# One 768 KB load of q cut in two, two softmax products on GpSimd, and a new order for the first two batches

## The chip, the cores and the metric

The kernel runs on one core of one Trainium2 chip. The metric is the device time of one launch in microseconds (us); the median of several launches is given. Kernels are compared only within the same rounds. A ratio is the mean time of one kernel's runs over that of the other's in the same rounds, so it is not quite the ratio of the medians quoted. Engines in the profile: PE is TensorE, DVE is VectorE, ACT is ScalarE, POOL is GpSimd, SP is SyncE, which only issues loads and stores here (SPq, ACTq: the issuing queues). The profiled span leaves out some 1.8 us of the launch.

## The reference, cut to what matters

```python
# q, k, v: (8 batches, 8 heads, 576, 64); w_in (512, 2048); w_out (2048, 512); beta (2048)
q_s = softmax(q over the 64 columns)          # exp, sum, divide
k_s = softmax(k over the 576 rows)
kv  = einsum('bhsd,bhse->bhde', k_s, v)
x   = einsum('bhsd,bhde->bhse', q_s, kv)      # then (8*576, 512)
h   = x @ w_in
out = (h / (1 + exp(-beta * h))) @ w_out
```

## The kernel before: what the change touches

The kernel is written in a manual order: each engine runs its instructions in the order of the program text. After a startup for batches 0 and 1 it goes through the batches with one long stream of matmuls, `h` (x times w_in) and `acc` (the gate's result times w_out), 0.216 us each. The eight heads of a batch are handled in four pairs, 0 to 3; q of one pair is 256 KB, k or v of one pair 288 KB.

```python
def load_q(b, parts=1, only=None, eng=nc.sync):      # parts `only` of b's heads, in 1 KB runs
    ...
    eng.dma_start(t[:, hs, :], src[:, hs, :])
def kz_exp(b, j):   # exponential of k, pair j of heads, on ScalarE
def vz_cast(b, j, eng, m=1, part=None):              # v to bf16
def q_exp(b, s, n): # ScalarE    def q_sum(b, s, n): # VectorE: sum, reciprocal
def q_mul(b, s, n=2, eng=nc.vector):                 # the softmax product
def tpe(b, j, tag): # 4 transposes on TensorE        def q_ev(b, j, eng): # copy out of PSUM
def kvz_mm(b, j, tag=None, n=1):                     # 18 small matmuls, k^T v of one pair
def xpe(c, j, tag): # x of one pair                  def hpe(c, j, kts): # h, one block of columns
def warm(n, tag):   # n dummy matmuls whose result nobody reads
...
load_q(0, 4, [0])                        # SyncE's queue, 256 KB
load_q(0, 4, [1, 2, 3], nc.scalar)       # ScalarE's queue, 768 KB
load_kv(k_st, k, 0, "k_st", whole=True)  # SyncE's queue, 1152 KB in 2.3 KB runs
load_kv(v_st, v, 0, "v_st", [0])         # 288 KB a pair
... # v's other pairs, beta (8 KB), w_in, w_out, batch 1
warm(18, tag="b0")
q_exp(0, 0, 4)
q_sum(0, 0, 4)
q_exp(0, 3, 4)
q_mul(0, 0, 4)
...
tpe(0, 0, "acc3")
...
warm(10, tag="acc2")
tpe(0, 2, "acc3")
... # some 215 more lines for batches 0 and 1
```

The softmax here doesn't subtract the row's maximum and nothing guards it: scores larger than these inputs give would overflow.

## Time and profile before

| | |
|---|---|
| median of 4 runs | 282.6 us (282.36 to 282.81) |
| profiled span | 280.75 us |
| first h matmul | 14.42 us |
| first h matmul to the first kv matmul of batch 2 | 46.74 us |
| from there to the end of the last matmul | 216.45 us |
| after it | 3.14 us |

The last four rows add up to the span. They come from the matmuls' times in the trace. The prediction below shows the profile's lines. In a row of digits, each digit is the busy share of one of 40 equal slices of the span, in tenths (9 is 90% or more). In a row of a timeline, the figures are start and length in us, then engine, line, operation, what is written and read, how many, and in brackets how long the engine sat idle before it and for whom it waited. Among the names, q_st, k_st and v_st are the loaded inputs, eq and ek their exponentials, rq the sums of q, va v in bf16, tp the transposes and w_in_b and w_out_b the weights in bf16. A load lands when the semaphore that tells of its end is seen.

### The profile page before, as it was taken

What the parts mean: (1) busy time and instruction counts of PE and PEld (TensorE: products, weight loads), DVE (VectorE), ACT (ScalarE), POOL (GpSimd) and SP (SyncE); (2) the same over time, 40 slices, a digit from 0 to 9 for tenths busy, and PEclk for the clock granted to TensorE, in tenths of its full rate; (3) what the DMA queues carried; (4) which work ended last, traced back from release to release, by engine and by line L of the source; (5) the groups of instructions that cost most, each with busy time, mean ns of one, the idle gap of its engine ahead of it and who ended that gap; (6) DMA issues with size and microseconds to landing.
All of it is one profiled execution on the core that took longest, in us unless ns stands there. A gap on an engine that the chain in (4) does not pass through costs nothing.

```text
span 280.8 us, 4419 instructions
## 1 busy us (share of the span) xinstructions
PE 273.9 (98%) x1699; PEld 128.2 (46%) x1728; DVE 175.3 (62%) x284; ACT 162.0 (58%) x248; POOL 38.7 (14%) x58
## 2 busy tenths in 40 slices
PE   8999999999999999999999999999999999999995
PEld 2644454444444444444444444444444544444543
DVE  3964786993498338934794469536964596354361
ACT  3767975953495439633873478337933574454451
POOL 1554237130030003000300030002100000000000
DMA  7999999929932994099309940698153034005003
GB/s 251 391 387 392 387 388 314 295 55 289 227 149 21 273 263 158 9 269 283 154 1 218 327 153 15 141 247 250 76 123 104 0 152 75 0 0 152 0 0 149
DMA packets 55172, 50.09 MB, mean 178 GB/s; under 512 B 26600, under 2 KB 47344, under 8 KB 55152
## 3 DMA queue, kind: packets, MB, share of 16 engines
q1 hardware_dynamic: 54224, 48.91, 58.3%
q10 hardware_dynamic: 928, 0.92, 0.9%
q8 instruction: 13, 0.21, 0.3%
q14 instruction: 7, 0.06, 0.1%
HBM read 36.71 MB, written 9.44 MB: 164 GB/s over the span
## 4 chain that ended last, share of the span: by engine, by line
PE 94%; DMA 3%; issue 1%; POOL 1%; SPq 0%; ACT 0%
PE h L398 44%; PE acc L446 43%; DMA v_st<-in_v_dram 3%; PE kv L339 2%; PE x L370 1%; PE acc L438 1%; PE kv L314 1%; PE x L383 1%; POOL va L171 1%; PE tp L295 0%; SPq L129 0%; SPq L106 0%; ACT o L169 0%; PE x L361 0%; PE tb L552 0%
## 5 line engine op out<-in xcount | busy, mean ns | idle before, releaser
L412 DVE SCALAR_TENSOR_TENSOR g<-th,h 128x512 bf16<-128x512 bf16 x144 | 97.0, 680 | 83.3 <-ACT th L408 81.4
L408 ACT ACTIVATE th<-h,beta_t 128x512 bf16<-128x512 f32 x144 | 97.9, 686 | 88.3 <-PE h L398 85.2
L398 PE MATMUL h<-xT,w_in_b 128*128 128x512 bf16 x569 | 141.0, 379 | 0.3
L446 PE MATMUL acc<-w_out_b,g 128*128 128x512 bf16 x538 | 136.3, 379 | 1.9 <-issue 1.1
L398 PEld LDWEIGHTS <-w_in_b 128*128 128x128 bf16 x576 | 56.3, 98 | 66.4 <-ACT w_in_b L169 0.6
L446 PEld LDWEIGHTS <-g 128*128 128x128 bf16 x560 | 53.4, 98 | 65.0 <-issue 2.5
L171 POOL CAST va<-v_st 128x2048 bf16<-128x2048 f32 (+2 forms) x14 | 17.5, 1261 | 145.7 <-DMA v_st<-in_v_dram 145.7
L259 DVE TENSOR_REDUCE rq<-eq 128x16 f32<-128x1024 bf16 (+1 forms) x20 | 22.1, 1105 | 5.6 <-ACT eq L248 5.2
L265 DVE TENSOR_TENSOR eq<-eq,rq 128x1024 bf16<-128x1024 bf16 (+1 forms) x20 | 22.8, 1142 | 0.1
L248 ACT ACTIVATE eq<-q_st 128x1024 bf16<-128x1024 f32 (+1 forms) x18 | 16.9, 956 | 3.2 <-DMA q_st<-in_q_dram 3.2
L169 ACT CAST xT<-x 128x512 bf16<-128x512 f32 x18 | 9.9, 588 | 12.1 <-PE x L370 10.1
L171 DVE CAST xT<-x 128x512 bf16<-128x512 f32 x18 | 11.6, 686 | 6.1 <-PE x L370 5.3
L171 DVE COPY o<-acc 128x512 f32<-128x512 f32 (+1 forms) x19 | 12.1, 670 | 3.3 <-PE acc L446 3.1
L169 ACT COPY o<-acc 128x512 f32<-128x512 f32 (+1 forms) x18 | 9.6, 576 | 7.5 <-PE acc L446 4.6
L190 ACT ACTIVATE ek<-k_st 128x1024 bf16<-128x1024 f32 x12 | 12.6, 1053 | 0.0
L519 PE MATMUL warm<-xT 128*128 128x512 bf16 x30 | 9.7, 483 | 1.2 <-DVE xT L600 1.2
L171 POOL CAST w_in_b<-w_in 128x512 bf16<-128x512 f32 (+1 forms) x9 | 5.9, 660 | 5.7 <-DMA w_in<-in_moe_w_in_dram 5.6
L519 PEld LDWEIGHTS <-xT 128*128 128x128 bf16 x30 | 3.4, 118 | 6.0 <-issue 3.5
L171 POOL CAST w_out_b<-w_out 128x1024 bf16<-128x1024 f32 x5 | 5.2, 1040 | 6.3 <-DMA w_out<-in_moe_w_out_dram 6.3
L183 ACT ACTIVATE ek<-k_st 128x576 bf16<-128x576 f32 x8 | 5.0, 674 | 0.6 <-DMA k_st<-in_k_dram 0.5
L260 DVE RECIPROCAL rq<-rq 128x16 f32<-128x16 f32 (+1 forms) x20 | 4.9, 243 | 0.7
L339 PEld LDWEIGHTS <-ek 128*64 128x64 bf16 x192 | 4.1, 111 | 2.5 <-issue 2.5
(48 smaller groups left out, 83.1 us busy)
## 6 DMA issues: line engine op xcount, KB each, us to landing
out_dram<-o SPq DMA_DIRECT2D x14, 512.0 KB, 3.4
q_st<-in_q_dram SPq DMA_DIRECT2D x25, 256.0 KB, 4.1
k_st<-in_k_dram SPq DMA_DIRECT2D x6, 1024.0 KB, 7.3
v_st<-in_v_dram SPq DMA_DIRECT2D x6, 1024.0 KB, 10.0
w_in<-in_moe_w_in_dram SPq DMA_DIRECT2D x6, 512.0 KB, 9.6
v_st<-in_v_dram SPq DMA_DIRECT2D x8, 288.0 KB, 8.4
w_out<-in_moe_w_out_dram SPq DMA_DIRECT2D x4, 512.0 KB, 8.8
w_out<-in_moe_w_out_dram SPq DMA_DIRECT2D x2, 1024.0 KB, 9.6
```

Source lines behind the costliest of these rows:

```text
L169: eng.copy(dst, src)
L171: eng.tensor_copy(dst, src)
L190: nc.scalar.activation(ek[b][:, :, h, :].rearrange("p i h d -> p h i d"), k_st[b][:, h, 0 : R * D].rearrange("p h (i d) -> p h i d", i=R), ...
L248: nc.scalar.activation(eq[b][:, :, s * m : (s + 1) * m, :].rearrange("p i h d -> p h i d"), q_st[b][:, s * m : (s + 1) * m, :].rearrange(" ...
L259: nc.vector.tensor_reduce(rq[b][:, 0, :, h], eq[b][:, :, h, :], axis=AX.X, op=ALU.add)
L265: eng.tensor_tensor(eq[b][:, :, h, :], eq[b][:, :, h, :], rq[b][:, 1, :, h].unsqueeze(3).to_broadcast((P, R, m, D)), ALU.mult,)
L339: nc.tensor.matmul(t[r * D : (r + 1) * D, j, :], ek[b][:, i, hd, :] if i < R else ekt[(b // 2) % 2][:, ds(hd * D, D)], va[b][:, i, hd, :] ...
L398: nc.tensor.matmul(h[:], w_unit(j, kt), x_of(c)[:, kt, :], start=(kt == 0), stop=(kt == KT - 1),)
L408: nc.scalar.activation(th[:], h_of[c, j][:], ACTF.Tanh, scale=beta_t[:, j : j + 1])
L412: nc.vector.scalar_tensor_tensor(out=g[:], in0=th_of.pop((c, j))[:], scalar=1.0, in1=h_of[c, j][:], op0=ALU.add, op1=ALU.mult)
L446: nc.tensor.matmul(acc[st][:], g[:, ds(st * P, P)], w_out_b[:, j, :], start=(j == 0), stop=(j == NJ - 1),)
L519: nc.tensor.matmul(t[:], xT[2][:, 0, 0:P], xT[2][:, 0, :])
```

## The change

Its intent: let the second pair of q land sooner, take two of VectorE's products to GpSimd, let two kv products of batch 1 share their normalisation, and reorder batches 0 and 1 around that. HB and AB in it name the memory banks that TensorE's results take in turn. The diff, cut to its core:

```diff
-    HB, AB = ["b1", "b2"], ["b0", "b3"]
+    HB, AB = ["b0", "b2"], ["b1", "b3"]
     load_q(0, 4, [0])
-    load_q(0, 4, [1, 2, 3], nc.scalar)
+    load_q(0, 4, [1], nc.scalar)
+    load_q(0, 4, [2, 3], nc.scalar)
     load_kv(k_st, k, 0, "k_st", whole=True)
     load_kv(v_st, v, 0, "v_st", [0])
+    nc.sync.dma_start(beta_r[:], ...)
+    load_kv(v_st, v, 0, "v_st", [2])
     load_kv(v_st, v, 0, "v_st", [1])
-    load_kv(v_st, v, 0, "v_st", [2])
-    nc.sync.dma_start(beta_r[:], ...)
 ...  (loads of w_in and of batch 1 in another order)
     q_exp(0, 0, 4)
+    q_exp(0, 1, 4)
     q_sum(0, 0, 4)
-    q_exp(0, 3, 4)
-    q_mul(0, 0, 4)
+    q_mul(0, 0, 4, eng=V)
+    q_exp(0, 2, 4)
+    q_sum(0, 1, 4)
+    q_exp(0, 3, 4)
+    tpe(0, 0, "acc3")
+    q_sum(0, 2, 4)
+    q_mul(0, 1, 4, eng=V)
+    q_mul(0, 2, 4, eng=G)
+    q_ev(0, 0, V)
+    warm(6, tag="acc1")
+    tpe(0, 1, "acc2")
 ...
+    q_mul(0, 3, 4, eng=G)
 ...  (the same steps of batch 0 in another order)
-    kvz_mm(1, 0, "b1", 1)
+    kvz_mm(1, 0, "b0", 2)
+    kvz_mm(1, 1)
+    kvz_norm(1, 0, 2)
 ...  (the same steps of batch 1 in another order)
```

More of the change, by code (lines that the diff above doesn't have):

```diff
@@ L562 @@
     load_q(0, 4, [0])
-    load_q(0, 4, [1, 2, 3], nc.scalar)
+    load_q(0, 4, [1], nc.scalar)
+    load_q(0, 4, [2, 3], nc.scalar)
     load_kv(k_st, k, 0, "k_st", whole=True)
     load_kv(v_st, v, 0, "v_st", [0])
+    nc.sync.dma_start(beta_r[:], moe_beta.rearrange("(hh q) -> hh q", q=2 * P))
+    load_kv(v_st, v, 0, "v_st", [2])
     load_kv(v_st, v, 0, "v_st", [1])
-    load_kv(v_st, v, 0, "v_st", [2])
-    nc.sync.dma_start(beta_r[:], moe_beta.rearrange("(hh q) -> hh q", q=2 * P))
     load_kv(v_st, v, 0, "v_st", [3])
@@ L571 @@
     w_load("in", 0, 1)
+    w_load("in", 1, 0)
     w_load("in", 0, 2)
     w_load("in", 0, 3)
-    w_load("in", 1, 0)
     w_load("in", 1, 1)
@@ L582 @@
     w_load("out", 1)
+    load_kv(v_st, v, 1, "v_st", [0])
+    load_kv(k_st, k, 1, "k_st", [0])
+    w_load("out", 2)
     load_q(1, 2, [0])
-    w_load("out", 2)
+    w_load("out", 3, 0)
     load_q(1, 2, [1])
-    load_kv(v_st, v, 1, "v_st", [2])
-    w_load("out", 3, 0)
-    load_kv(k_st, k, 1, "k_st", [0])
-    load_kv(v_st, v, 1, "v_st", [0])
-    load_kv(k_st, k, 1, "k_st", [2])
-    load_kv(k_st, k, 1, "k_st", [1])
-    load_kv(v_st, v, 1, "v_st", [1])
-    w_load("out", 3, 1)
-    load_kv(k_st, k, 1, "k_st", [3])
+    load_kv(v_st, v, 1, "v_st", [1])
+    load_kv(k_st, k, 1, "k_st", [1])
+    w_load("out", 3, 1)
+    load_kv(k_st, k, 1, "k_st", [2])
+    load_kv(k_st, k, 1, "k_st", [3])
+    load_kv(v_st, v, 1, "v_st", [2])
     load_kv(v_st, v, 1, "v_st", [3])
@@ L608 @@
     q_exp(0, 0, 4)
+    q_exp(0, 1, 4)
     q_sum(0, 0, 4)
+    q_mul(0, 0, 4, eng=V)
+    q_exp(0, 2, 4)
+    q_sum(0, 1, 4)
     q_exp(0, 3, 4)
-    q_mul(0, 0, 4)
-    q_exp(0, 2, 4)
-    q_sum(0, 3, 4)
-    tpe(0, 0, "acc3")
-    q_exp(0, 1, 4)
-    q_sum(0, 2, 4)
-    q_ev(0, 0, A)
-    q_sum(0, 1, 4)
-    q_mul(0, 2, 4)
+    tpe(0, 0, "acc3")
[5 more added lines that the diff above has]
+    tpe(0, 1, "acc2")
+    q_sum(0, 3, 4)
@@ L620 @@
     kz_exp(0, 0)
-    q_mul(0, 1, 4)
-    warm(10, tag="acc2")
+    warm(1, tag="acc1")
     tpe(0, 2, "acc3")
+    q_ev(0, 1, V)
+    q_mul(0, 3, 4, eng=G)
+    q_ev(0, 2, A)
+    warm(1, tag="acc0")
+    beta_pe("acc1")
     kz_exp(0, 1)
-    q_ev(0, 2, V)
+    vz_cast(0, 2, A, part=1)
     vz_cast(0, 0, G)
-    warm(1, tag="acc1")
-    tpe(0, 1, "acc2")
-    q_mul(0, 3, 4)
+    warm(3, tag="acc0")
+    tpe(0, 3, "acc3")
     kz_exp(0, 2)
-    warm(1, tag="acc1")
-    kvz_mm(0, 0, "acc3", 1)
+    vz_cast(0, 2, G, part=0)
@@ L633 @@
+    q_ev(0, 3, A)
+    warm(1, tag="acc0")
+    kvz_mm(0, 0, "acc2", 1)
     vz_cast(0, 1, G)
-    q_ev(0, 1, V)
-    tpe(0, 3, "acc1")
+    kvz_mm(0, 2, "acc0", 1)
     kz_exp(0, 3)
     kvz_norm(0, 0)
-    kvz_mm(0, 1, "acc2", 1)
-    vz_cast(0, 2, G)
-    q_ev(0, 3, A)
-    beta_pe("acc0")
-    kvz_norm(0, 1)
-    kvz_mm(0, 2, "acc3", 1)
-    vz_cast(0, 3, A, part=1)
-    vz_cast(0, 3, G, part=0)
-    beta_ev()
-    xpe(0, 0, "acc1")
-    kvz_norm(0, 2)
-    kvz_mm(0, 3, "acc2", 1)
-    w_castk(0, 0, G)
+    vz_cast(0, 3, G)
@@ L651 @@
+    warm(1, tag="b3")
+    kvz_mm(0, 1, "acc3", 1)
+    beta_ev()
+    kvz_norm(0, 2)
+    w_castk(0, 0, A)
+    xpe(0, 0, "acc2")
+    kvz_norm(0, 1)
+    kvz_mm(0, 3, "acc1", 1)
     xev(0, 0, A)
-    xpe(0, 1, "acc0")
+    w_castk(0, 1, G)
+    xpe(0, 2, "acc0")
     kvz_norm(0, 3)
-    xpe(0, 2, "b3")
+    xpe(0, 1, "b3")
+    xev(0, 2, A)
+    hpe(0, 1, [0], "b0")
+    hpe(0, 0, [0], "b1")
     xev(0, 1, A)
-    hpe(0, 0, [0], "b0")
-    hpe(0, 1, [0], "b1")
-    xev(0, 2, V)
-    w_castk(0, 1, A)
+    hpe(0, 2, [0], "b2")
@@ L660 @@
+    w_castk(1, 1, G)
     xpe(0, 3, "acc3")
-    w_castk(0, 2, G)
-    hpe(0, 3, [0], "b2")
-    xev(0, 3, V)
-    hpe(0, 2, [0], "acc0")
+    hpe(0, 3, [0], "acc0")
+    xev(0, 3, A)
+    hpe(0, 1, [1])
+    w_castk(1, 0, G)
     hpe(0, 0, [1])
+    hpe(0, 2, [1])
+    w_castk(0, 2, A)
+    hpe(0, 3, [1])
     w_castk(0, 3, G)
-    hpe(0, 3, [1])
-    hpe(0, 3, [2])
-    hpe(0, 1, [1])
+    hpe(0, 7, [0], "b3")
+    hpe(0, 4, [0], "acc1")
+    hpe(0, 0, [2])
+    hpe(0, 0, [3])
+    hpe(0, 2, [2])
@@ L670 @@
+    th_act(0, 0)
+    hpe(0, 4, [1])
+    hpe(0, 3, [2])
+    w_castk(1, 3, G)
+    hpe(0, 3, [3])
+    hpe(0, 2, [3])
+    g_dve(0, 0)
+    w_castk(1, 2, G)
+    th_act(0, 3)
+    hpe(0, 7, [1])
     hpe(0, 1, [2])
     hpe(0, 1, [3])
-    hpe(0, 3, [3])
-    th_act(0, 1)
-    w_castk(1, 0, G)
-    hpe(0, 0, [2])
-    hpe(0, 0, [3])
-    hpe(0, 2, [1])
-    w_castk(1, 1, G)
-    th_act(0, 3)
-    hpe(0, 2, [2])
-    g_dve(0, 1)
-    hpe(0, 2, [3])
-    hpe(0, 4, [0], "b3")
-    th_act(0, 0)
-    hpe(0, 4, [1])
@@ L686 @@
-    g_dve(0, 3)
-    w_castk(1, 3, G)
-    hpe(0, 5, [0], "b1")
-    hpe(0, 5, [1])
-    w_castk(1, 2, A)
-    g_dve(0, 0)
-    hpe(0, 7, [0], "b2")
-    th_act(0, 2)
-    hpe(0, 7, [1])
-    hpe(0, 4, [2])
-    hpe(0, 5, [2])
+    th_act(0, 2)
+    hpe(0, 7, [2])
+    g_dve(0, 3)
+    hpe(0, 4, [2])
+    hpe(0, 5, [0], "b1")
+    th_act(0, 1)
     hpe(0, 4, [3])
     g_dve(0, 2)
-    hpe(0, 5, [3])
-    th_act(0, 4)
-    hpe(0, 7, [2])
-    hpe(0, 7, [3])
-    hpe(0, 6, [0], "b0")
-    w_cast("out", 0, 0, G)
+    hpe(0, 7, [3])
@@ L705 @@
+    w_cast("out", 0, 0, G)
+    hpe(0, 5, [1])
+    th_act(0, 4)
+    g_dve(0, 1)
+    hpe(0, 5, [2])
+    hpe(0, 5, [3])
+    th_act(0, 7)
+    hpe(0, 6, [0], "b2")
+    g_dve(0, 4)
+    hpe(0, 6, [1])
+    hpe(0, 6, [2])
     th_act(0, 5)
-    hpe(0, 6, [1])
-    g_dve(0, 4)
-    hpe(0, 6, [2])
+    w_cast("out", 0, 1, G)
     hpe(0, 6, [3])
-    th_act(0, 7)
-    g_dve(0, 5)
+    g_dve(0, 7)
     mm_b(0, 0)
     th_act(0, 6)
-    w_cast("out", 0, 1, G)
-    g_dve(0, 7)
+    g_dve(0, 5)
     mm_b(0, 1)
+    w_castk(2, 0, G)
@@ L717 @@
     g_dve(0, 6)
-    w_castk(2, 0, A)
     w_castk(2, 1, G)
     mm_b(0, 2)
-    mm_b(0, 3)
     w_castk(2, 2, A)
     w_castk(2, 3, G)
-    hpe(0, 11, [0, 1, 2, 3], "b0")
+    mm_b(0, 3)
+    hpe(0, 8, [0, 1, 2, 3], "b0")
     w_cast("in", 3, 1, A)
     hpe(0, 10, [0, 1, 2, 3], "b1")
+    th_act(0, 8)
+    w_cast("in", 3, 0, G)
+    hpe(0, 11, [0, 1, 2, 3], "b2")
+    th_act(0, 10)
+    g_dve(0, 8)
+    hpe(0, 9, [0, 1, 2, 3], "b3")
+    g_dve(0, 10)
     th_act(0, 11)
-    hpe(0, 8, [0, 1, 2, 3], "b2")
@@ L729 @@
-    w_cast("in", 3, 0, G)
-    th_act(0, 10)
+    hpe(0, 13, [0, 1, 2, 3], "b0")
     g_dve(0, 11)
-    hpe(0, 9, [0, 1, 2, 3], "b3")
-    th_act(0, 8)
-    g_dve(0, 10)
-    hpe(0, 13, [0, 1, 2, 3], "b0")
-    g_dve(0, 8)
     th_act(0, 9)
-    hpe(0, 14, [0, 1, 2, 3], "b1")
+    w_cast("out", 1, 0, G)
+    hpe(0, 12, [0, 1, 2, 3], "b1")
     g_dve(0, 9)
     th_act(0, 13)
-    w_cast("out", 1, 0, G)
-    w_cast("out", 1, 1, A)
-    hpe(0, 15, [0, 1, 2, 3], "b2")
-    g_dve(0, 13)
-    mm_b(0, 4)
@@ L746 @@
-    th_act(0, 14)
-    th_act(0, 15)
-    g_dve(0, 14)
-    mm_b(0, 5)
-    q_exp(1, 0)
-    g_dve(0, 15)
-    mm_b(0, 6)
-    q_sum(1, 0)
-    mm_b(0, 7)
-    w_cast("out", 2, 1, A)
-    w_cast("out", 2, 0, G)
-    hpe(0, 12, [0, 1, 2, 3], "b0")
-    q_mul(1, 0)
-    q_exp(1, 1)
-    mm_b(0, 8)
-    vz_cast(1, 2, G, part=0)
-    vz_cast(1, 2, A, part=1)
-    mm_b(0, 9)
-    q_sum(1, 1)
-    th_act(0, 12)
-    tpe(1, 0, "b1")
-    w_cast("out", 3, 0, A)
-    tpe(1, 1, "b2")
-    mm_b(0, 10)
-    q_ev(1, 0, V)
@@ L771 @@
-    q_mul(1, 1)
-    kz_exp(1, 0)
-    mm_b(0, 11)
-    vz_cast(1, 0, G, part=0)
-    vz_cast(1, 0, A, part=1)
-    q_ev(1, 1, A)
-    g_dve(0, 12)
-    kvz_mm(1, 0, "b1", 1)
-    kz_exp(1, 2)
-    tpe(1, 3, "b3")
-    kvz_norm(1, 0)
-    tpe(1, 2, "b2")
-    mm_b(0, 12)
-    kz_exp(1, 1)
-    q_ev(1, 3, V)
-    q_ev(1, 2, V)
-    kvz_mm(1, 2, "b0", 1)
-    vz_cast(1, 1, A, part=1)
-    vz_cast(1, 1, G, part=0)
-    xpe(1, 0, "b1")
-    kvz_norm(1, 2)
-    kvz_mm(1, 1, "b2", 1)
-    xev(1, 0, A)
@@ L794 @@
-    mm_b(0, 13)
-    kvz_norm(1, 1)
-    w_cast("out", 3, 1, G)
-    hpe(1, 0, [0], "b0")
-    xpe(1, 2, "b1")
-    kz_exp(1, 3)
-    xpe(1, 1, "b2")
-    xev(1, 2, V)
-    mm_b(0, 14)
+    vz_cast(1, 0, A, part=1)
+    hpe(0, 14, [0, 1, 2, 3], "b2")
+    w_cast("out", 1, 1, G)
+    g_dve(0, 13)
+    th_act(0, 12)
+    kz_exp(1, 0)
+    mm_b(0, 4)
+    g_dve(0, 12)
+    vz_cast(1, 0, G, part=0)
+    th_act(0, 14)
+    mm_b(0, 5)
+    g_dve(0, 14)
+    mm_b(0, 6)
+    w_cast("out", 2, 0, G)
+    mm_b(0, 7)
@@ new lines @@
+    w_cast("out", 2, 1, G)
+    mm_b(0, 8)
+    q_exp(1, 0)
+    mm_b(0, 9)
+    q_sum(1, 0)
+    w_cast("out", 3, 0, G)
+    mm_b(0, 10)
+    mm_b(0, 11)
+    q_mul(1, 0, eng=V)
+    q_exp(1, 1)
+    mm_b(0, 12)
+    vz_cast(1, 1, G)
+    q_sum(1, 1)
+    mm_b(0, 13)
+    kz_exp(1, 1)
+    tpe(1, 0, "b0")
+    tpe(1, 1, "b1")
+    q_ev(1, 0, V)
+    hpe(0, 15, [0, 1, 2, 3], "b2")
+    q_ev(1, 1, A)
+    w_cast("out", 3, 1, G)
+    q_mul(1, 1, eng=V)
+    kvz_mm(1, 0, "b0", 2)
+    kz_exp(1, 2)
@@ L803 @@
+    kvz_mm(1, 1)
+    th_act(0, 15)
+    tpe(1, 2, "b1")
+    kvz_norm(1, 0, 2)
+    tpe(1, 3, "b3")
+    mm_b(0, 14)
+    q_ev(1, 2, A)
+    q_ev(1, 3, V)
+    vz_cast(1, 2, G)
+    kz_exp(1, 3)
+    g_dve(0, 15)
+    xpe(1, 0, "b0")
+    xpe(1, 1, "b1")
     vz_cast(1, 3, A, part=1)
     vz_cast(1, 3, G, part=0)
+    kvz_mm(1, 2, "b3", 1)
     xev(1, 1, V)
-    kvz_mm(1, 3, "b1", 1)
+    xev(1, 0, A)
+    kvz_mm(1, 3, "b2", 1)
     mm_b(0, 15)
+    kvz_norm(1, 2)
     kvz_norm(1, 3)
-    hpe(1, 2, [0], "b2")
+    xpe(1, 2, "b0")
@@ L810 @@
     store(0, 0)
-    xpe(1, 3, "b1")
+    hpe(1, 0, [0], "b1")
+    xev(1, 2, V)
+    hpe(1, 0, [1])
+    xpe(1, 3, "b2")
     hpe(1, 1, [0], "b3")
+    store(0, 1)
+    xev(1, 3, A)
     hpe(1, 1, [1])
-    xev(1, 3, A)
-    store(0, 1)
     hpe(1, 1, [2])
-    hpe(1, 0, [1])
     hpe(1, 0, [2])
@@ L821 @@
     hpe(1, 1, [3])
-    hpe(1, 3, [0], "b1")
+    hpe(1, 2, [0], "b0")
     th_act(1, 0)
     store(0, 3)
-    hpe(1, 3, [1])
-    hpe(1, 3, [2])
-    hpe(1, 3, [3])
-    th_act(1, 1)
-    g_dve(1, 0)
     hpe(1, 2, [1])
     hpe(1, 2, [2])
+    th_act(1, 1)
+    hpe(1, 2, [3])
+    g_dve(1, 0)
+    hpe(1, 3, [0], "b2")
+    hpe(1, 3, [1])
+    th_act(1, 2)
+    hpe(1, 3, [2])
+    g_dve(1, 1)
+    hpe(1, 3, [3])
+    mm_b(1, 0)
     th_act(1, 3)
-    hpe(1, 2, [3])
-    g_dve(1, 1)
-    mm_b(1, 0)
-    th_act(1, 2)
+    g_dve(1, 2)
+    mm_b(1, 1)
     g_dve(1, 3)
-    mm_b(1, 1)
-    g_dve(1, 2)
     tail_zero(0)
```

## The prediction

> **What bounds the kernel now.** I read, in this order: the busy shares and slices of the page, the chain of work that ended last (first 20 us), and each engine's timeline over the first 25 us and over 25 to 50 us, since the diff touches only batches 0 and 1.
>
> ```profile
> PE 273.9 (98%) x1699; PEld 128.2 (46%) x1728; DVE 175.3 (62%) x284; ACT 162.0 (58%) x248; POOL 38.7 (14%) x58
> ...
> PE   8999999999999999999999999999999999999995
> ...
> DMA  7999999929932994099309940698153034005003
> ```
>
> See: TensorE is at nine tenths or more in every slice between the first and the last; the DMA engines are full for the first eight slices (7 us each, so to 56 us).
>
> ```profile
> 1.74 8.15 DMA v_st<-in_v_dram
> 9.95 2.12 POOL va L171 x2
> ...
> 12.11 0.48 PE kv L314 x18
> ...
> 14.86 0.38 PE x L383
> 15.23 3.96 PE h L398 x18
> ```
>
> See: until 12.1 us the end hangs on the first loads of v and on two GpSimd casts (2.12 us together); from 12.11 us on the chain is TensorE's own work.
>
> ```profile
> 1.19 6.67 PE L519 MATMUL warm<-xT 128*128 128x512 bf16 x18 [1.19 <-DVE xT L600]
> 7.69 0.39 PE L295 MATMUL tp<-identity,eq 128*128 128x128 bf16 x4
> 7.92 2.32 PE L519 MATMUL warm<-xT 128*128 128x512 bf16 x10
> ...
> 12.11 0.48 PE L314 MATMUL kv<-va,ek 64*64 64x65 bf16 x18
> ...
> 14.42 0.38 PE L398 MATMUL h<-xT,w_in_b 128*128 128x512 bf16 x1
> ...
> 15.07 6.88 PE L398 MATMUL h<-xT,w_in_b 128*128 128x512 bf16 x30
> ```
>
> See: 28 of the first matmuls are dummies (warm). No idle bracket stands behind any later row. In the chain four matmuls of 512 columns take 0.86 us, so 0.216 us each; the rows from 25.24 to 46.83 us hold 86 such (18.6 us), 16 transposes (0.9) and 72 kv matmuls (1.6): 21.1 of 21.6 us. So batch 1's startup has at most 0.5 us to give back, and the rest of the time can only fall if TensorE begins its real work before 12.1 us.
>
> ```profile
> 3.79 0.63 ACT L248 ACTIVATE eq<-q_st 128x512 bf16<-128x512 f32 x1 [1.25 <-DMA q_st<-in_q_dram]
> 6.13 1.67 ACT L248 ACTIVATE eq<-q_st 128x512 bf16<-128x512 f32 x3 [1.70 <-DMA q_st<-in_q_dram]
> ...
> 9.18 2.40 ACT L183 ACTIVATE ek<-k_st 128x576 bf16<-128x576 f32 x4 [0.48 <-DMA k_st<-in_k_dram]
> ...
> 9.95 3.11 POOL L171 CAST va<-v_st 128x576 bf16<-128x576 f32 x4 [7.99 <-DMA v_st<-in_v_dram]
> ```
>
> See: the landings. q in two steps (3.8 and 6.1 us), k at 9.2, v's first pair at 9.9; v's later pairs land at 10.6, 11.4 and 12.15 by their semaphores in the trace.
>
> **What the Trainium skill says.** "DMA: Bandwidth & Descriptors", section "Issuing engines are not separate DMA queues": loads issued from several engines run on the same 16 DMA engines and interleave. The trace agrees on the sum (390 GB/s from 2.5 us on, whatever queue), so splitting a load moves no later landing forward: the last v still lands near 12.1 us. But it does not interleave finely here: the first packet of q's 768 KB from ScalarE's queue starts at 2.63 us, k's first on the other queue only at 5.03 us though it was issued at 1.24 us. Loads went one after the other in order of issue. "GPSIMD Engine Reference", section "3.1 Elementwise — side-by-side cycle accounting": a two-input product costs about 2.6 cycles an element. With 512 elements at 1.2 GHz I estimate 1.1 us and a little dispatch, 1.2 us, against 0.69 us for the same product on VectorE in the trace; the kernel before has no such GpSimd product. "SBUF — State Buffer", section "Who interferes with whom": a VectorE instruction with two SBUF inputs blocks a GpSimd instruction that reads SBUF. The trace agrees: the two GpSimd casts beside VectorE's products and copies took 1.02 and 1.14 us, the next of the same shape 0.66 us.
>
> **The change, part by part.** (1) q of batch 0 comes as 256, 256 and 512 KB. Pair 1 should land near 4.2 us instead of 6.1 (256 KB at 0.39 MB per us is 0.7 us behind the first's last packets at 3.4, and 0.1 to 0.4 us to the semaphore). If the last 512 KB still goes ahead of k, pairs 2 and 3 land at 6.1 as before. (2) Two of four products go to GpSimd. (3) Pair 2's v is loaded before pair 1's and its cast is split with ScalarE, so that VectorE and GpSimd are less in the way. (4) All four casts of x are on ScalarE now. (5) Dummies: 31 for 30, no cost while TensorE waits anyway; one (0.216 us) stands between kv products.
>
> Placing the new order by the durations of before, with q landing at 3.8, 4.2 and 6.1:
> VectorE: sums and product of pair 0 to 6.1 as before; sum of pair 1 to 6.85; of pair 2 6.8 to 7.7; product of pair 1 to 8.3; sum of pair 3 to about 9.45.
> GpSimd: product of pair 2 held up by VectorE's to about 8.3, then to 9.5; product of pair 3 9.5 to 10.7; casts of v: pair 0 10.7 to 11.35 (before: 10.97), half of pair 2 to 11.75, pair 1 to 12.4, pair 3 to 13.0.
> ScalarE: k exponential 0 at 9.18, copy of transpose 2 at 10.05, exponential 1 at 10.55, half cast at 11.1, exponential 2 at 11.55 to 12.15, copy at 12.1, exponential 3 at 12.6 to 13.2, beta, weight cast to 13.9, then x casts 0, 2, 1, 3 end at 14.4, 15.0, 15.5, 16.0.
> TensorE: kv of pair 0 at 11.45, pair 2 at 12.2, pair 1 at 12.85, x0 13.25, pair 3 13.55, x2 14.0, x1 14.2, h from 14.5, with one wait of about 0.1 us at 15.5 for x1's cast.
> By 17.1 us this gives 4 x and 11 h matmuls; before, (17.1 - 15.13)/0.216 = 9 plus 2 of 14.4 to 14.9, so 11 h as well. The startup gain is nil: what the early q gains is in front of v's landing, which didn't move, and GpSimd's two products (2.4 us) use it up. I charge +0.1 us, with 0.3 either way.
>
> Batch 1: kv of pairs 0 and 1 lie side by side, with one reciprocal for two: VectorE saves three small instructions of 0.17 to 0.23 us, off the path. Two switches fewer between 512-column matmuls and kv (starts 0.31 us apart where 0.216 is usual in the trace) give 2 x 0.09 = 0.2 us. Against it, v of pairs 2 and 3 now lands last (42.5 to 43.8 us by the same total of bytes) and kv of pairs 2 and 3 is due near 43.9: cast of 0.5 to 1.1 us, so a wait of 0.1 to 0.4 us. Sum -0.2 + 0.25: nil. From batch 2 on, both kernels have the same instructions. Total: 282.59 + 0.1 - 0.2 + 0.25, rounded down for slack that the order search may have used better than my placing: 282.5.
>
> **The rivals.** (a) k overtakes the last 512 KB of q: both are issued at about 1.25 us on different queues. The serial order of issue speaks for a coin toss; that the new order has VectorE go straight from the sum of pair 1 to that of pair 2 says its author saw q land in time. Then pairs 2 and 3 land near 9.1 us (the same bytes as q and k together before), the sum of pair 2 runs at 9.8, GpSimd's products end at 11.9 and 13.6, four v casts end near 15.9 instead of 13.06, and kv of pair 3 comes at 16.0 instead of 13.57: +2.4 us, 285.0. If the two interleave evenly, q lands near 6.9 and it costs some 0.6 us, 283.2. I give them 0.25 and 0.1. (b) GpSimd's products run as fast as VectorE's, with fewer lock waits: the casts begin at 9.95, kv 2 starts at 11.6 and TensorE is dense 0.5 us sooner; with batch 1's 0.3 us this gives 281.8. A rate of 1 element per ns in GpSimd's casts speaks for it, the second operand against it. (c) A wait for x1 or for weight columns spreads, as w_in is cast by a later GpSimd: +0.5 us; TensorE's 16 matmuls a weight block (3.45 us) against 2.7 us a block of DMA speaks against it.
>
> **Range and chances.** The mean of the main case is 282.5 with 0.4 either way; 281.8 is its low end with (b). The high end 284.9 takes in most of (a). 2% is 5.65 us: no gain can reach it, as the dummies and waits before 12.1 us are bound by loads that don't move; a loss of it needs twice rival (a). Hence faster 0.01, same 0.97, slower 0.02.
>
> **What would show it.** Right: exponentials of q pairs at 3.8, 4.3, 6.1; GpSimd's products 1.1 to 1.3 us each; first cast of v at about 10.7; h matmuls without gaps from 14.5; kv of batch 1's pair 2 with a short wait on GpSimd near 44 us; TensorE's distance from 50 us to the end unchanged. Wrong: q's third exponential at 7 or 9 us; products under 0.8 us; x casts on ScalarE that hold TensorE for over 0.3 us; any change of pace after 50 us.

## The result, and the profile after

The changed kernel takes 287.44 us (median of 4, 286.88 to 287.59) against 282.6 us: ratio 1.0168, 95% interval 1.015 to 1.0186. It is 4.8 us slower, outside the range that I gave.

| stretch, us | before | after | difference |
|---|---|---|---|
| start to the first h | 14.42 | 19.88 | +5.46 |
| first h to the first kv of batch 2 | 46.74 | 46.07 | -0.67 |
| from there to the last matmul | 216.45 | 216.45 | 0 |
| after it | 3.14 | 3.25 | +0.11 |

All of the loss is in front of the first h. The page of the changed kernel, with the granted clock of TensorE as a new row (it is printed where it was not full throughout):

```profile
PE 276.9 (97%) x1729; PEld 128.7 (45%) x1729; DVE 171.5 (60%) x276; ACT 159.3 (56%) x245; POOL 43.7 (15%) x64
...
PE   8499999999999999999999999999999999999995
...
PEclk9779999999999999999999999999999999999999
DMA  7999999917950895169527942489344033005003
```

TensorE is more than half idle in the second slice (7 to 14 us), and its clock is below full in the second and third. The clock records of the trace say 0.5 (half of the full clock) from 10.72 to 17.55 us. The chain of work that ended last, first 22 us of the changed kernel:

```profile
1.26 8.85 DMA q_st<-in_q_dram
...
10.14 0.64 ACT eq L248
...
10.80 0.70 DVE rq L259
...
12.43 0.58 PE tp L295 x4
13.01 0.43 PE warm L519
13.44 0.43 PE tp L295 x4
13.86 0.43 PE warm L519
...
14.62 1.39 PE warm L519 x3
16.02 0.43 PE tp L295 x4
16.44 0.43 PE warm L519
16.87 0.99 PE kv L314 x19
```

Before, the chain began with v and its casts. Now it begins with q: a load issued at 1.26 us that takes 8.85 us to land. From 12.43 us it is TensorE itself at half clock, 0.43 us for a dummy instead of 0.216, with six dummies in the chain in front of the first kv. ScalarE and TensorE, timelines of the changed kernel:

```profile
0.74 1.02 ACTq L106 DMA_DIRECT2D q_st<-in_q_dram  x2
...
4.04 1.15 ACT L248 ACTIVATE eq<-q_st 128x512 bf16<-128x512 f32 x2 [0.96 <-DMA q_st<-in_q_dram]
10.14 1.15 ACT L248 ACTIVATE eq<-q_st 128x512 bf16<-128x512 f32 x2 [4.95 <-DMA q_st<-in_q_dram]
11.19 0.67 ACT L183 ACTIVATE ek<-k_st 128x576 bf16<-128x576 f32 x1
13.90 0.59 ACT L169 COPY qsT<-tp 128x512 bf16<-128x512 bf16 x1 [2.04 <-PE tp L295]
```

```profile
6.72 1.46 PE L519 MATMUL warm<-xT 128*128 128x512 bf16 x6
12.43 0.58 PE L295 MATMUL tp<-identity,eq 128*128 128x128 bf16 x4 [4.25 <-DVE eq L265]
...
20.74 5.56 PE L398 MATMUL h<-xT,w_in_b 128*128 128x512 bf16 x25
```

Pairs 0 and 1 of q arrive by 4.34 us, as intended. Pairs 2 and 3 arrive at 10.12 us instead of 6.1, ScalarE waits 4.95 us for them, and k, which landed at 8.75 us, has to wait behind them in ScalarE's order.

Why so late? I counted the DMA packets of the trace that ended in half a microsecond, by queue (q1: SyncE's, q10: ScalarE's) and size:

```
from     before                                   after
4.0 us   q10: 189 of 1 KB                         q1: 91 of 2.3 KB (k)
5.0      q10: 70 of 1 KB, q1: 38 of 2.3 KB        q1: 53 of 2.3 KB, q10: 57 of 1 KB
6.0      q1: 86 of 2.3 KB (k)                     q1: 56, q10: 53
7.0      q1: 85                                   q1: 58, q10: 57
8.0      q1: 86                                   q1: 58, q10: 55
```

In the kernel before, q's 768 KB went first and k's packets began (5.03 us) when they were nearly done. In the changed kernel the two queues take turns, with about as many packets each. "DMA: Bandwidth & Descriptors", section "Queues, rings and completion order", of the Trainium skill says that an engine goes round its queues packet by packet. The changed kernel agrees (57 to 53 packets), if a packet of the page, which can hold several of the trace's, holds as many in both queues. The kernel before does not show it between q's 768 KB and k, though both loads had been issued by 1.7 us. It does show it between q's own two loads, both issued at 0.74 us: from 2.63 to 3.37 us 149 packets of one and 105 of the other ended. Turn about by packet is not half and half by bytes: k's packet is 2.3 KB and q's is 1 KB, so q gets some 57 KB of 180 in half a microsecond, a third. Its 512 KB then need about 4.5 us from 4.5 us on, and the semaphore followed at 10.12 us.

### The profile page after: what moved, and what is told of

It is laid out like the page before. It is cut to its first block, busy times and chain, and to the rows that moved or that the text cites. A ratio compares the mean times of both kernels' runs of the same rounds, so it can differ in the third digit from the quotient of the medians.

```text
span 285.6 us, 4443 instructions
## 1 busy us (share of the span) xinstructions
PE 276.9 (97%) x1729; PEld 128.7 (45%) x1729; DVE 171.5 (60%) x276; ACT 159.3 (56%) x245; POOL 43.7 (15%) x64
## 4 chain that ended last, share of the span: by engine, by line
PE 95%; DMA 3%; DVE 1%; ACT 0%; ACTq 0%; issue 0%
PE h L398 44%; PE acc L446 43%; DMA q_st<-in_q_dram 3%; PE kv L339 2%; PE x L370 1%; PE acc L438 1%; PE kv L314 1%; PE warm L519 1%; PE tp L295 1%; PE x L383 1%; DVE rq L259 0%; ACT eq L248 0%; DVE eq L265 0%; ACTq L106 0%; ACT o L169 0%
## 5 line engine op out<-in xcount | busy, mean ns | idle before, releaser
L446 PE MATMUL acc<-w_out_b,g 128*128 128x512 bf16 x560 | 139.0, 379 | 0.0
L265 DVE TENSOR_TENSOR eq<-eq,rq 128x1024 bf16<-128x1024 bf16 (+1 forms) x18 | 20.8, 1155 | 0.1
L169 ACT CAST xT<-x 128x512 bf16<-128x512 f32 x20 | 10.9, 588 | 12.0 <-PE x L370 10.1
L171 DVE CAST xT<-x 128x512 bf16<-128x512 f32 x16 | 10.4, 686 | 5.3 <-PE x L370 5.3
L519 PE MATMUL warm<-xT 128*128 128x512 bf16 x31 | 10.6, 479 | 1.2 <-DVE xT L601 1.2
L171 POOL CAST w_out_b<-w_out 128x1024 bf16<-128x1024 f32 x8 | 8.2, 1042 | 5.8 <-DMA w_out<-in_moe_w_out_dram 5.7
L295 PE MATMUL tp<-identity,eq 128*128 128x128 bf16 x32 | 3.5, 252 | 4.3 <-DVE eq L265 4.3
L169 ACT COPY qsT<-tp 128x512 bf16<-128x512 bf16 x4 | 2.3, 586 | 6.1 <-PE tp L295 5.9
## 6 DMA issues: line engine op xcount, KB each, us to landing
v_st<-in_v_dram SPq DMA_DIRECT2D x6, 1024.0 KB, 10.7
```

Source lines behind the costliest of these rows:

```text
L169: eng.copy(dst, src)
L171: eng.tensor_copy(dst, src)
L265: eng.tensor_tensor(eq[b][:, :, h, :], eq[b][:, :, h, :], rq[b][:, 1, :, h].unsqueeze(3).to_broadcast((P, R, m, D)), ALU.mult,)
L295: nc.tensor.transpose(tp_of[b, j][:, i, :], eq[b][:].rearrange("p i (j x) d -> p i j (x d)", j=HP)[:, i, j, :], identity[:],)
L446: nc.tensor.matmul(acc[st][:], g[:, ds(st * P, P)], w_out_b[:, j, :], start=(j == 0), stop=(j == NJ - 1),)
L519: nc.tensor.matmul(t[:], xT[2][:, 0, 0:P], xT[2][:, 0, :])
```

## The experiments

My theory L: q's third load, issued at 1.26 us in the same moment as k's at 1.25 us, shares with k and lands 4 us late. With it goes theory C: the idle TensorE loses its clock on top. Rivals: the two GpSimd products in front of v's casts (G), and the new orders themselves (O). "Before" is the median of the kernel before.

| kernel | median us | before | ratio, 95% interval |
|---|---|---|---|
| the change | 287.44 | 282.6 | 1.0168 (1.015 to 1.0186) |
| two_loads | 283.01 | 282.58 | 1.0012 (0.9997 to 1.0026) |
| q23_first | 283.85 | 282.58 | 1.0039 (1.0024 to 1.0054) |
| split_only | 289.54 | 282.58 | 1.0231 (1.0198 to 1.0263) |
| warm_more | 285.84 | 282.58 | 1.011 (1.0093 to 1.0127) |
| beta_first | 283.97 | 282.75 | 1.0052 (1.0037 to 1.0067) |
| v_products | 283.15 | 282.75 | 1.0017 (1.0003 to 1.003) |
| stall_fix | 282.9 | 282.75 | 1.0007 (0.9995 to 1.002) |
| b1_only | 282.66 | 282.75 | 1.0001 (0.9989 to 1.0014) |
| b1_lock | 282.61 | 282.72 | 0.9999 (0.9985 to 1.0012) |
| split_warm | 286.67 | 282.72 | 1.014 (1.0126 to 1.0154) |
| tie_one_load | 290.91 | 282.56 | 1.0279 (1.0246 to 1.0311) |

All gave correct results.

### two_loads: the change without its third load

```diff
-    load_q(0, 4, [1], nc.scalar)
-    load_q(0, 4, [2, 3], nc.scalar)
+    load_q(0, 4, [1, 2, 3], nc.scalar)
```

> The changed kernel with q of batch 0 back in two loads (256 KB, and 768 KB as one issue on ScalarE's queue); all orders, the two GpSimd products and the dummies stay. Theory L (the third load of q is issued beside k's and the two share the DMA engines, so q's pairs 2 and 3 land at 10.1 us instead of 6.1): q lands at about 6.1 us again, TensorE's clock never drops, time 282.0 to 282.8, so all of the 4.8 us is back. Rival G (the two products on GpSimd, 1.31 and 1.05 us, in front of the casts of v are the cost): time stays within 1.5 us of the changed kernel, 286 or more. Rival O (the new orders themselves): the same, 286 or more.

283.01 us: 4.4 of the 4.8 us are gone, with both products still on GpSimd and all new orders in place. L holds; G and O fall as the main cause. q landed at 5.92 us and the clock stayed full. ScalarE's timeline of two_loads:

```profile
5.94 1.67 ACT L248 ACTIVATE eq<-q_st 128x512 bf16<-128x512 f32 x3 [1.34 <-DMA q_st<-in_q_dram]
```

The rest, 0.4 us, is not clear of noise: the interval takes in no difference. Still, 283.01 us is 0.2 us above the 282.0 to 282.8 that I had written, and TensorE's timeline of two_loads shows one more wait:

```profile
15.61 3.83 PE L398 MATMUL h<-xT,w_in_b 128*128 128x512 bf16 x16
20.23 2.77 PE L398 MATMUL h<-xT,w_in_b 128*128 128x512 bf16 x12 [0.79 <-POOL w_in_b L171]
```

A half of w_in's second block landed at 18.94 us in this run, and GpSimd cast its two rows one after the other until 20.2 us. Before, GpSimd and ScalarE did one each.

### split_only: the kernel before, with q in three loads and nothing else

```diff
-    load_q(0, 4, [1, 2, 3], nc.scalar)
+    load_q(0, 4, [1], nc.scalar)
+    load_q(0, 4, [2, 3], nc.scalar)
```

> The kernel before with nothing but q in three loads as the change has it. Theory L: the third load lands near 10.1 us here too; exponentials of pairs 3, 2 and 1 start at 10.1 and kv of pair 0 near 15 us instead of 11.07: 285.5 to 287.0, slower than before by 3 to 4.5 us. Rivals G and O: within 0.5 us of before.

289.54 us, +7.0 us: the split alone does more harm than the whole change. The third load landed at 10.67 us, as L says. My number was too low by 2.5 us. I had not counted TensorE's clock: the records show 0.5 from 12.38 to 22.62 us. Whether that is the reason is tested by split_warm, below. TensorE's timeline of split_only:

```profile
14.56 0.59 PE L295 MATMUL tp<-identity,eq 128*128 128x128 bf16 x4 [4.80 <-ACT ek L183]
```

### q23_first: three loads, the third in front of k on the same queue

```diff
     load_q(0, 4, [1], nc.scalar)
-    load_q(0, 4, [2, 3], nc.scalar)
+    load_q(0, 4, [2, 3])
```

> The changed kernel, still with three loads, but the third (pairs 2 and 3) is issued on SyncE's queue between q's first load and k's, so that it stands before k in the same queue. Theory L: pair 1 lands at about 4.3 us and pairs 2 and 3 at about 6.2, k at 9.2, and the time is 281.8 to 282.6, a little below two_loads (within 0.4 us). If the number of loads as such costs, 284 or more. Rival G: 286 or more.

Pairs 2 and 3 landed at 5.95 us and the time is 283.85 us, 3.6 us better than the change. So three loads as such are not the main harm. But I expected 281.8 to 282.6, and the interval leaves a loss of 0.7 to 1.5 us. k landed at 10.03 us and v's first pair at 10.77, where the kernels with two loads and the change's order of batch 0 have 8.94 to 9.56 and 9.69 to 10.29. Why k is later here I have not settled. The trace also shows that TensorE waited 0.85 us, until 11.09 us, for the 8 KB of beta, which were issued behind the other loads at 2.84 us and landed at 10.95 us.

### beta_first: the third load stays where it is, k is issued 0.43 us later

```diff
+    nc.sync.dma_start(beta_r[:], ...)      # 8 KB, moved up
     load_kv(k_st, k, 0, "k_st", whole=True)
     load_kv(v_st, v, 0, "v_st", [0])
-    nc.sync.dma_start(beta_r[:], ...)
```

> The changed kernel, three loads as they are, with the tiny beta load (8 KB) moved in front of k's on SyncE's queue, so that k is issued about 0.45 us after q's third load instead of in the same moment. Theory S (what decides is which of the two issues is first; the later waits behind the earlier, as k did behind q's 768 KB in the kernel before): q's pairs 2 and 3 land near 6.2 us, the half clock never comes, time 282.5 to 283.5, as two_loads. Theory R (two queues that both have work share packet by packet whenever they are both full): q's third load still lands at 9 to 10 us and the time stays at 286.5 or more.

SyncE's and ScalarE's timelines of beta_first:

```profile
1.24 0.40 SPq L565 DMA_DIRECT2D beta_r<-in_moe_beta_dram  x1
1.69 0.40 SPq L129 DMA_DIRECT2D k_st<-in_k_dram  x1
```

```profile
4.03 1.15 ACT L248 ACTIVATE eq<-q_st 128x512 bf16<-128x512 f32 x2 [0.95 <-DMA q_st<-in_q_dram]
6.36 1.15 ACT L248 ACTIVATE eq<-q_st 128x512 bf16<-128x512 f32 x2 [1.19 <-DMA q_st<-in_q_dram]
10.00 0.68 ACT L183 ACTIVATE ek<-k_st 128x576 bf16<-128x576 f32 x1 [2.49 <-DMA k_st<-in_k_dram]
```

An 8 KB issue in front of k moves q's third landing from 10.12 to 6.34 us and the time from 287.44 to 283.97 us. Between 4.0 and 4.5 us 188 packets of q ended and none of k. R falls: with 0.43 us between the issues q's load goes alone, as S says of the load that is issued first. The time is 0.5 us above what I had written, and k is late (9.98 us) as in q23_first.

### tie_one_load: the kernel before, with q's 768 KB issued beside k

```diff
+    nc.scalar.dma_start(beta_r[:], ...)    # 8 KB, in front of q on ScalarE's queue
     load_q(0, 4, [1, 2, 3], nc.scalar)
...
-    nc.sync.dma_start(beta_r[:], ...)
```

> The kernel before (q in two loads, its own orders) with the 8 KB beta load moved in front of q's 768 KB on ScalarE's queue, so that the 768 KB are issued near 1.2 us, in the same moment as k on SyncE's queue, instead of 0.5 us ahead of it. Theory S (the same moment of issue is what makes the two share packet by packet; the number of loads of q is not it): k and q alternate, q's 1 KB packets get some 30% of the bytes, and q's last three pairs land at 9 to 10.5 us instead of 6.1; TensorE idles, its clock may drop, and the time is 285 to 290. Rival N (it takes three loads of q): q lands near 6.4 us and the time stays within 1 us of before.

ScalarE's timeline of tie_one_load:

```profile
0.74 0.59 ACTq L563 DMA_DIRECT2D beta_r<-in_moe_beta_dram  x1
1.36 0.42 ACTq L106 DMA_DIRECT2D q_st<-in_q_dram  x1
...
12.42 1.67 ACT L248 ACTIVATE eq<-q_st 128x512 bf16<-128x512 f32 x3 [8.07 <-DMA q_st<-in_q_dram]
```

q is loaded as in the kernel before and only issued 0.62 us later (1.36 instead of 0.74), k as ever at 1.24 us. From 6.0 to 10.5 us the queues took turns (for instance 58 packets of k or v against 59 of q from 6.0), q landed at 12.40 us and the time is 290.91 us, +8.3 us, half clock from 13.57 to 23.81 us included. Landing and time are both above what I had written (9 to 10.5 us, and 285 to 290). The run rules out N: the harm needs no third load, only q's big load issued 0.12 us after k's instead of 0.5 us before it.

A rival to "the same moment" stays open: the order. In every run in which the two shared, k's packets began first (in the change at 3.59 us, q's third load at 4.50; in tie_one_load 2.73 and about 3.5). In every run in which q went alone, q's packets began first (in the kernel before at 2.63 us, k's at 5.03). No run issued k well ahead of q, so these runs don't tell whether the short gap or k's being first makes them share. S, that the later load waits behind the earlier, is shown only for q ahead of k.

### warm_more: 18 more dummies in the idle gap of the changed kernel

```diff
-    warm(6, tag="acc1")
+    warm(24, tag="acc1")
```

> The changed kernel with 24 dummies instead of 6 behind the first transposes, 18 x 0.216 = 3.9 us, which fill TensorE's idle 4.25 us from 8.2 to 12.4. Theory C (the idle gap drops TensorE's clock to half from 10.72 to 17.55 us, and the transposes and six dummies on the path run at 0.43 us each): the granted clock stays at 1.0 and the time falls by 0.8 to 2.0 us to 285.4 to 286.6. If the half clock lies off the path, the time stays within 0.3 us of 287.4.

285.84 us, 1.6 us faster than the change with 3.9 us more of useless work. The clock stayed at 1.0. TensorE's timeline of warm_more:

```profile
7.32 5.34 PE L519 MATMUL warm<-xT 128*128 128x512 bf16 x24
12.51 0.38 PE L295 MATMUL tp<-identity,eq 128*128 128x128 bf16 x4
12.72 0.38 PE L519 MATMUL warm<-xT 128*128 128x512 bf16 x1
```

The transposes come at the same time as in the change (12.51 against 12.43 us) and what follows is faster: kv starts at 15.38 instead of 16.80 us. Theory C holds, with 1.6 us. "TensorE: Matmul & The Clock Gate", section "What's actually happening", of the Trainium skill gives half clock after an idle window of about 3.4 us. The gap here, 4.25 us, is longer than that, but by the records the clock fell 2.54 us after the last dummy (8.18 and 10.72 us), in split_only 2.61 us and in tie_one_load 3.22 us: less than 3.4 us without a matmul was enough.

### split_warm: 20 more dummies in the idle gap of split_only

```diff
-    warm(10, tag="acc2")
+    warm(30, tag="acc2")
```

> split_only with 30 dummies instead of 10 behind the first transposes (20 x 0.216 = 4.3 us), which fill the idle 4.8 us of TensorE that came with the late third load. Theory C: split_only was slower than I had expected (289.5 against 285.5 to 287.0) because the half clock lasted from 12.4 to 22.6 us there, over the kv products, the x products and the first h. With the gap filled the clock stays at 1.0 and the time falls by 2 to 4 us, to 285.5 to 287.5. If the half clock is not the reason, it falls by less than 1 us.

286.67 us, 2.9 us faster than split_only, with a full clock. So the clock was the part of split_only that I had not counted; 286.67 lies in the 285.5 to 287.0 that I had first written for split_only.

### v_products: two_loads with the products back on VectorE

```diff
-    q_mul(0, 2, 4, eng=G)
+    q_mul(0, 2, 4, eng=V)
...
-    q_mul(0, 3, 4, eng=G)
+    q_mul(0, 3, 4, eng=V)
```

> two_loads (q in two loads, the change's orders) with the two products of batch 0 on VectorE instead of GpSimd. Theory: GpSimd's products (1.31 and 1.05 us) set the first cast of v to 11.17 us where v had landed at 9.7; without them the casts begin at about 9.8 and kv of pair 0 comes up to 1 us sooner, but ScalarE's chain of k exponentials and copies still sets kv of pair 2 and 3, so the gain in time is 0.1 to 0.4 us: 282.6 to 282.9. If the products had been the cost of the start alone: 282.2 or less. If VectorE becomes the bound: 283.2 or more.

283.15 us, 0.4 us over its kernel before as two_loads was over its own. The first cast of v came at 10.04 us instead of 11.17, but kv of pair 0 at 12.50 instead of 11.90, as k landed 0.3 us later in this run and a transpose stood in front. I had written 282.6 to 282.9, a gain of 0.1 to 0.4 us; there is none. GpSimd's products cost nothing that I can resolve, and gain nothing.

### stall_fix: two_loads with one weight cast back on ScalarE

```diff
-    w_castk(1, 2, G)
+    w_castk(1, 2, A)
```

> two_loads with the cast of w_in block 1's third row block back on ScalarE, as in the kernel before. In two_loads TensorE waits 0.79 us at 19.4 us for two such casts done one after the other by GpSimd (19.0 to 20.2). Two engines side by side end near 19.6: wait shorter by 0.4 to 0.6 us, time 282.4 to 282.7. If the wait is only moved (ScalarE's tanh of block 3 comes later): within 0.15 us of two_loads.

TensorE's wait fell from 0.79 to 0.16 us in the profile. The time, 282.9 us, has an interval that takes in both no difference from before and 0.2%. I had written 282.4 to 282.7. I call it unclear: in the profiled run k landed 0.6 us later than in two_loads and the first h came 0.36 us later, so the two spans are the same (281.4 us).

### b1_only and b1_lock: the change's batch 1 on the old batch 0

b1_only is the kernel before up to the last matmul that block 0 of w_out needs (`mm_b(0, 3)`), with the change's loads and order from there. It asks where the 0.67 us went that the changed kernel is shorter by after its first h.

> The kernel before up to the second product of block 0 (its loads, orders, no GpSimd product), then the change's loads and orders of batch 1. In the traces, from the first dense h matmuls to the end the changed kernel takes 0.5 us less than before. If that gain is the batch 1 orders' own: 281.9 to 282.4, faster than before by 0.2 to 0.7 us. If it only came from the later start (loads of batch 1 relatively earlier): within 0.15 us of before, or slower.

282.66 us, the same as before: the gain is not there. VectorE of b1_only:

```profile
40.19 0.42 DVE L171 COPY qsT<-tp 128x512 bf16<-128x512 bf16 x1
40.53 2.03 DVE L265 TENSOR_TENSOR eq<-eq,rq 128x1024 bf16<-128x1024 bf16 x1
```

GpSimd of b1_only, and TensorE of b1_only:

```profile
40.44 1.04 POOL L171 CAST w_out_b<-w_out 128x1024 bf16<-128x1024 f32 x1 [1.26 <-DMA w_out<-in_moe_w_out_dram]
```

```profile
42.62 0.62 PE L295 MATMUL tp<-identity,eq 128*128 128x128 bf16 x8 [0.68 <-DVE eq L265]
```

GpSimd's cast begins 0.09 us before VectorE's product, which then takes 2.03 us, and TensorE waits 0.68 us. b1_lock moves that cast:

```diff
-    w_cast("out", 3, 1, G)
     q_mul(1, 1, eng=V)
     ...
     kz_exp(1, 2)
+    w_cast("out", 3, 1, A)
```

> b1_only with the last w_out cast of GpSimd (1.04 us) moved to ScalarE, behind the exponential of batch 1's third pair. In b1_only VectorE's product of batch 1's second half took 2.03 us where its twin took 1.23, while GpSimd's cast ran from 40.44 to 41.48, and TensorE then waited 0.68 us for it. Theory P (the two block each other over SBUF): the product takes 1.2 us again, TensorE's wait falls to under 0.1 us, and the time is 281.8 to 282.3, faster than before by 0.3 to 0.8 us. If the product's length has another cause, it stays near 2 us and the time within 0.15 us of before; if ScalarE's cast holds up its copies, a wait appears on ScalarE and the time is 282.4 or more.

VectorE of b1_lock:

```profile
40.88 1.22 DVE L265 TENSOR_TENSOR eq<-eq,rq 128x1024 bf16<-128x1024 bf16 x1
```

The product takes 1.22 us again and TensorE's wait is gone; the stretch from the first h to batch 2 falls from 46.97 us (b1_only) to 46.56 us. Theory P is right about the mechanism. The time is 282.61 us, the same as before, so my 281.8 to 282.3 was wrong: a gain of 0.2 us against the old 46.74 us is under what these runs resolve, when the landing of k alone moves by 0.3 us between profiled runs. I found no version that is faster than the kernel before.

## Why the prediction was wrong

I had said that the time would stay within 2% of before, and it did, but by luck: the same late load without the change's orders (split_only) cost 7.0 us, 2.3% (interval 2.0 to 2.6%). The range was wrong, and the reason is one step.

**The step that failed: the landing of q's last 512 KB.** The main case let this load go ahead of k and land at 6.1 us; it landed at 10.12 us. The prediction read the kernel before as "Loads went one after the other in order of issue". That was true of q's 768 KB and k, issued 0.5 us apart, and I took it for a rule. The same trace showed q's own two loads, issued at the same moment, taking turns, and I overlooked it. In rival (a) I called it a coin toss who goes first, gave 0.1 to interleaving, and then sized interleaving at "q lands near 6.9" by sharing the bytes evenly. The trace shows sharing by packet, with a third of the bytes for q, and a landing later than even in the case in which k goes first (9.1 us): k's queue went on with v when k was done (from 8.5 to 9.5 us 126 packets of 2.3 KB against 75 of q). beta_first and tie_one_load show that the times of issue decide it, on the same queues and with the same big loads. The size was wrong as well as the weight. And the range ended at 284.9, just short of rival (a) itself at 285.0, to which I had given 0.25; it did not "take in most of (a)". A loss of 2% (5.65 us) would have needed 2.4 times rival (a), not twice. The 390 GB/s "from 2.5 us on" is a little high too: the packets give 366 GB/s from 2.5 to 7 us.

**A term that was missing: the clock.** The prediction knew 28 dummies and did not ask what TensorE does when 6 of them stand where 10 stood and the next product is late. The gap of 4.25 us, itself due to the late q, cost 1.6 us more (warm_more) in dummies and transposes at half clock on the path. The sum by experiments: 287.44 - 285.84 = 1.6 us clock, 285.84 - 283.01 = 2.8 us late q itself, 283.01 - 282.58 = 0.4 us the rest, which is not clear of noise; together 4.8 us.

**VectorE's sums.** They ran about as placed up to the sum of pair 1 (it ended near 7.2 us, placed at 6.85) and then stood until 10.80 us, because the order goes straight to pair 2, which the prediction took as a sign that the order's author saw q land in time. That an order suits an early landing is no evidence of the landing.

**GpSimd's products**: 1.31 and 1.05 us against 1.1 to 1.3 written. Right in size, and right that they don't set the time: with q early, the first cast of v was at 11.17 us (10.7 written), and v_products showed nothing to win.

**The startup with q in time**: 14.74 us to the first h in two_loads against 14.5 written. Right within 0.3 us. The wait for weights at 19 us (0.79 us) was rival (c), which I sized at 0.5 and judged unlikely.

**Batch 1**: I wrote nil (-0.2 and +0.25). In the changed kernel, which starts late, the stretch after the first h is 0.67 us shorter; in b1_lock, with the old start, 0.2 us remain. How much of the 0.67 us is batch 0's was not separated. The wait that I named (for v's cast near 44 us) did not come: the changed kernel shows no wait of TensorE between 40 and 52 us. b1_only has one of 0.68 us, for VectorE's product, which a GpSimd cast held up. And from batch 2 on the pace was the same to 0.01 us, as written.

**Still open**: why k and v land 0.4 to 1.1 us later when all three q loads go ahead of k (q23_first, beta_first). By 8.5 us 539 packets of 2.3 KB (k's and v's) had ended in beta_first and 538 in two_loads, so there the DMA engines together were not behind; in q23_first it was 466. Open too is what q needs to go alone: leads of 0.43 and 0.5 us over k were enough, leads of 0.00 (split_warm), -0.02 (the change) and -0.12 us (tie_one_load) were not, and nothing between, nor k far ahead, was tried.

## What to carry to other kernels

When two queues each hold a large load, look at the issue times: loads issued within 0.12 us of each other shared packet by packet here, and the one with the smaller packets then lost; a small issue in front of the less urgent one, or the same queue for both, gave the order back. Splitting a load to have its first part early also moves the issue of its last part, so check what that now ties with. And price an idle TensorE with its clock: a gap of 4 to 5 us cost another 1.6 to 2.9 us here, which dummies in the gap won back.

## What the Trainium skill lacked or had wrong

- "DMA: Bandwidth & Descriptors", section "Queues, rings and completion order": the round by packets agrees with the runs in which both issues fell together (57 packets to 53), but the page doesn't say that a load issued 0.43 to 0.5 us ahead on another queue can go alone (188 packets to 0, q ahead of k), nor that the split of bytes follows the packet size (1 KB against 2.3 KB: q's 512 KB landed at 10.12 instead of 6.34 us).
- The same page, section "Issuing engines are not separate DMA queues": it says that issuing from several engines only saves issue time. Here it also set the order of landing: the same third load of q landed at 10.12 us from ScalarE's queue and at 5.95 us from SyncE's, in front of k, and the time moved by 3.6 us (the change against q23_first).
- "TensorE: Matmul & The Clock Gate", section "What's actually happening": it gives full clock after about 3.4 us of busy array. In split_only TensorE started again at 14.56 us with transposes, small kv matmuls and single dummies, and full clock came at 22.62 us, 8.1 us later, more than two such windows, though TensorE was busy throughout from 15.79 to 19.21 us; in the change it took 5.1 us (12.43 to 17.55 us). For half clock the page gives an idle window of that length; here the clock fell 2.5 to 3.2 us after the last matmul. The stretch also differed between launches: three launches of split_only had a mean clock of 0.982 (10.2 us at half in the profiled one), the fastest (287.85 us) 0.988, which I estimate as 7 us at half.
- "GPSIMD Engine Reference", section "3.1 Elementwise — side-by-side cycle accounting": nothing wrong; my estimate from its rate was 1.1 us, and the runs show 1.05 and 1.31 us for a 128x512 product.
- "SBUF — State Buffer", section "Who interferes with whom": nothing wrong; it says that a VectorE instruction with two SBUF inputs contends with a GpSimd instruction that reads SBUF, and in b1_only a product of 1.22 us took 2.03 us beside a GpSimd cast of 1.04 us that had begun 0.09 us sooner.
